# A feed-forward kernel's second matmul by one level of Strassen's algorithm: seven half-size products on summed blocks for eight

## The chip, the core and the metric

The kernel runs on one core of one Trainium2 chip. The metric is device time in microseconds, the median over executions. The profile names the engines PE (TensorE, matmul; PEld is its weight load), DVE (VectorE), ACT (ScalarE), POOL (GpSimd) and SP (SyncE, whose queue issues most DMAs here). Each engine works through its own instructions in order and waits on semaphores for the others.

## What is computed

```python
def _attn_ref(q, k, v):                 # (8, 8, 576, 64) each
    q_s = softmax of q over the head dimension
    k_s = softmax of k over the sequence
    kv = np.einsum('bhsd,bhse->bhde', k_s, v)
    return np.einsum('bhsd,bhde->bhse', q_s, kv)

def _moe_ref(x, w_in, w_out):           # x (4608, 512), w_in (512, 2048), w_out (2048, 512)
    h = x @ w_in
    g = 0.5 * h * (1.0 + erf(h / sqrt(2)))
    return g @ w_out
```

The attention's output, heads side by side, is x: 8 batches of 576 tokens, 512 wide. Inputs and output are fp32 in HBM; the kernel computes in bf16 with fp32 sums in PSUM.

## The kernel before

The tokens go in nine **chunks** of M = 512: chunks 0 to 7 are the first 512 tokens of each batch, chunk 8 the 64 that are left over of each. A chunk has three matmul parts on TensorE:

- **x**: `x_mm` multiplies the normalized queries, transposed (`qT`), with the batch's small matrix `kvc`; four copies (`x_evac`, two on ACT, two on DVE) put x, transposed, into `xT`.
- **h**: `h_phase` makes 16 tiles of h, transposed (128 of the 2048 hidden columns by 512 tokens), each of four matmuls of 512 columns (L348); ACT writes its GELU into `g` (L354), `[128, 16, 512]` bf16. `g` has one buffer.
- **y**: `y_phase` goes over four groups `j` of 128 tokens. For each, 16 matmuls of 512 columns (L376) sum over the hidden tiles `t`, with a block of `g` as weights and a row block of `wo_bf` (w_out in bf16) streaming. DVE copies each bank out (`y_out`, L384) and SP stores it. For chunk 8 the last group is done by `y_last` in 384 and 128 columns (L401), and its stores go out in halves of 64 rows, by SP and ACT.

The order of instructions on every engine is the order in the source (a manual schedule). What prepares a later chunk is put between matmuls of the y phase by the dict `ins`, whose keys are `(j, t)`. In chunks 2 to 5 the y phase of chunk c holds, for the batch nb = c + 2: `cast_v_all(nb)` (four DVE casts of V, L169) at (0, 8); `norm_q(nb)` at (1, 0), which is a reduce and a reciprocal on DVE and a multiplication on POOL (L245); `xbar_step(nb)` at (3, 0), a transposing DMA on SP's queue that makes `qT`; and at (2, 12) `x_all(c + 1)`, the x part of the next chunk, and `kv_step(nb)`, the k-times-v matmuls (L206) and their normalization on DVE. ACT does the exponentials of batch nb in the y phase as well. The loads of q, k and v for nb are issued by SP at the start of the h phase of chunk c. Chunk 6 has `norm_q` and the transpose only, for the left-over queries; chunks 7 and 8 prepare nothing but x for chunk 8.

The first part is written out by hand: weights are loaded in fp32 into five rotating buffers (`wst`) and cast to bf16 by DVE, POOL and ACT while chunk 0 runs; chunk 0's y phase is interleaved with the attention of batch 1, and the first four h tiles of chunk 1 are written out (`hps`). POOL's work there is casts and half of `norm_q(1)`.

PSUM has eight banks: three rotate for h (`psum_h`), two for y (`psum_y`), one (`a`) and a pair (`a2`) serve the attention.

Of the kernel before, what the change touches and what calls it, by code (L numbers as in the profile page):

```python
# [16 lines left out]
def kernel(  # L17
# [308 lines left out]
    def x_all(b):

        for hp in range(HP):
            pool, tag = (psum_h, "h") if hp < 3 else (psum_a, "a")
            x_tile(b, hp, pool, tag)  # L330
# [12 lines left out]
    def h_begin(c):  # L343
        st[c]["g"] = moe_sb.tile([128, NDF, M], BF16, tag="g", name="g", bufs=1)

    def h_mm(c, ps, t, dms):
        for dm in dms:
            nc.tensor.matmul(  # L348
                ps, wi_bf[:, dm, t * 128:(t + 1) * 128], st[c]["xT"][:, dm, :],
                start=(dm == 0), stop=(dm == NDM - 1),  # L350
            )
# [23 lines left out]
    def y_mm(c, ps, j, t):  # L375
        nc.tensor.matmul(  # L376
            ps, st[c]["g"][:, t, j * 128:(j + 1) * 128], wo_bf[:, t, :],
            start=(t == 0), stop=(t == NDF - 1),
        )

    def y_out(c, ps, j, eng="v"):
        y_sb = moe_sb.tile([128, DM], FP32, tag="y_sb")
        if eng == "v":
            nc.vector.tensor_copy(out=y_sb, in_=ps)  # L384
        else:
            nc.scalar.copy(out=y_sb, in_=ps)
        if c < B:
            dst = out[c * S:c * S + M, :].rearrange("(p j) n -> p j n", j=J)[:, j, :]
            nc.sync.dma_start(out=dst, in_=y_sb)
        else:  # L390
            for b2 in range(2):
                r0 = (2 * j + b2) * S + M
                nc.sync.dma_start(out=out[r0:r0 + R, :], in_=y_sb[b2 * R:(b2 + 1) * R, :])

    def y_last():

        j = J - 1
        for i, (c0, n) in enumerate(((0, 384), (384, 128))):
            ps = psum_y.tile([128, DM], FP32, tag="y")
            for t in range(NDF):  # L400
                nc.tensor.matmul(  # L401
                    ps[:, 0:n], st[B]["g"][:, t, j * 128:(j + 1) * 128],
                    wo_bf[:, t, c0:c0 + n], start=(t == 0), stop=(t == NDF - 1),
                )
            y_sb = moe_sb.tile([128, DM], FP32, tag="y_sb")
            nc.vector.tensor_copy(out=y_sb[:, 0:n], in_=ps[:, 0:n])  # L406
            for b2 in range(2):
                r0 = (2 * j + b2) * S + M
                eng = nc.scalar if b2 else nc.sync
                eng.dma_start(  # L410
                    out=out[r0:r0 + R, c0:c0 + n], in_=y_sb[b2 * R:(b2 + 1) * R, 0:n]
                )

    def y_phase(c, ins):
        for j in range(J - 1 if c == B else J):
            ps = psum_y.tile([128, DM], FP32, tag="y")
            for t in range(NDF):
                y_mm(c, ps, j, t)
                for f in ins.get((j, t), []):
                    f()  # L420
            y_out(c, ps, j)
        if c == B:
            y_last()
# [301 lines left out]
```

## Time and profile before

| what | us |
|---|---|
| median of 3 runs (279.41 to 279.45) | 279.44 |
| span of the profiled execution | 277.5 |
| PE busy in that span | 270.9 |
| one h phase, 64 matmuls of 512 columns | 13.81 |
| one y phase of chunks 2 to 5, with x and kv | 15.12 |
| y phase of chunk 1 (58.09 to 74.02) | 15.93 |
| y phase of chunk 8 to the end of the span (260.23 to 277.5) | 17.3 |

The profile is of one execution; its own time runs from its first to its last instruction, and the runs' median lies 1.94 us above that span. The granted TensorE clock is full in all slices of the page. A row of a group reads: line, engine, operation, output from input, shapes, count, then busy time and the mean of one, then the idle time of the engine just before and who ended it. A row of the timeline reads: start, duration, engine, line and operation, and in brackets how long the engine had been idle and for whom. In the chain, a row is start, length, what ran. Names are the program's; `e` is the exponential of q, `f` a loaded fp32 tile, `ps` a PSUM bank.

### The profile page before, as it was taken

The page shows a single profiled execution, that of the slowest core. Times are in us where ns is not written, and L with a number is a line of the kernel's source. Part 1 is how long each engine was busy: PE and PEld are TensorE (multiplying, and loading weights), DVE is VectorE, ACT ScalarE, POOL GpSimd, SP SyncE. Part 2 cuts the span into 40 slices and gives each one's busy share as a digit, 9 for nine tenths or more (in the row PEclk, how much of TensorE's full clock was granted, in tenths as well). Part 3 has the DMA queues.
Part 4 walks back from the last instruction along what each step waited for, and adds up shares of the span by engine and source line. Part 5 has one row for each costly group of instructions (what it writes and reads, how often), then busy time and mean ns, then how long its engine had stood idle before and what let it go on. Part 6 is the DMA issues. An engine that isn't in the chain of part 4 may idle for free.

```text
span 277.5 us, 4658 instructions
## 1 busy us (share of the span) xinstructions
PE 270.9 (98%) x1966; PEld 125.6 (45%) x1966; DVE 100.8 (36%) x154; ACT 158.9 (57%) x247; POOL 32.5 (12%) x26
## 2 busy tenths in 40 slices
PE   7799999999999999999999999999999999999995
PEld 3344454444444444444444444444444444444443
DVE  2876565319743540263008400751015200120012
ACT  4867686689377717791669246943683363126400
POOL 1520041002020310013000500050005000000000
PEclk9999999999999999999999999999999999999999
DMA  7999999974993249613981189117402500220033
GB/s 258 400 374 427 402 400 404 400 271 116 312 307 64 77 109 297 239 40 94 268 320 38 53 215 398 56 41 193 109 0 78 151 0 0 78 76 0 2 76 77
DMA packets 44980, 50.10 MB, mean 181 GB/s; under 512 B 20384, under 2 KB 29856, under 8 KB 44704
## 3 DMA queue, kind: packets, MB, share of 16 engines
q1 hardware_dynamic: 44560, 49.39, 53.5%
q10 hardware_dynamic: 400, 0.43, 0.5%
q8 instruction: 15, 0.25, 0.4%
q14 instruction: 5, 0.04, 0.1%
HBM read 36.70 MB, written 9.44 MB: 166 GB/s over the span
## 4 chain that ended last, share of the span: by engine, by line
PE 94%; DMA 4%; POOL 0%; DVE 0%; issue 0%; SPq 0%
PE ps L348 44%; PE ps L376 44%; DMA f<-in_v_dram 2%; PE kv L206 2%; PE ps L315 2%; DMA f<-in_q_dram 2%; PE ps L401 1%; PE pair L348 1%; POOL v_aug L169 0%; PE ps L320 0%; PE tp L279 0%; SPq L103 0%; DVE kvc L225 0%; DVE y_sb L406 0%; DVE rec L224 0%
## 5 line engine op out<-in xcount | busy, mean ns | idle before, releaser
L348 PE MATMUL ps<-xT,wi_bf 128*128 128x512 bf16 x568 | 124.9, 379 | 0.0
L376 PE MATMUL ps<-wo_bf,g 128*128 128x512 bf16 x560 | 124.1, 379 | 0.0
L354 ACT ACTIVATE g<-ps 128x512 bf16<-128x512 f32 x142 | 83.5, 598 | 66.8 <-PE ps L348 66.7
L348 PEld LDWEIGHTS <-wi_bf 128*128 128x128 bf16 x576 | 56.2, 98 | 68.0 <-issue 0.8
L376 PEld LDWEIGHTS <-g 128*128 128x128 bf16 x560 | 54.0, 98 | 64.6 <-issue 0.4
L384 DVE COPY y_sb<-ps 128x512 f32<-128x512 f32 x33 | 22.7, 687 | 81.0 <-PE ps L376 80.7
L245 POOL TENSOR_TENSOR e<-e,recq 128x2048 bf16<-128x2048 bf16 (+1 forms) x9 | 25.7, 2855 | 175.9 <-DVE recq L244 141.2
L169 DVE CAST v_aug<-f 128x576 bf16<-128x576 f32 x24 | 16.4, 746 | 48.3 <-DMA f<-in_v_dram 48.3
L243 DVE TENSOR_REDUCE qsum<-e 128x16 f32<-128x1024 bf16 (+1 forms) x13 | 21.1, 1622 | 13.7 <-ACT e L152 13.6
L341 ACT CAST xT<-ps 128x512 bf16<-128x512 f32 x18 | 9.9, 588 | 26.4 <-PE ps L315 15.9
L152 ACT ACTIVATE e<-f 128x512 bf16<-128x512 f32 (+1 forms) x42 | 20.5, 556 | 3.5 <-DMA f<-in_q_dram 3.5
L157 ACT ACTIVATE ek<-f 128x2304 bf16<-128x2304 f32 (+1 forms) x10 | 17.2, 1728 | 0.6 <-DMA f<-in_k_dram 0.5
L339 DVE CAST xT<-ps 128x512 bf16<-128x512 f32 x17 | 11.0, 687 | 17.1 <-PE ps L315 14.1
L79 ACT ACT_TABLE_LOAD x9 | 11.5, 1283 | 2.8 <-issue 2.7
L494 PE MATMUL ps<-zeros 128*128 128x512 f32 x14 | 8.0, 734 | 1.5 <-DVE zeros L520 1.5
L152 ACT ACT_TABLE_LOAD x7 | 9.0, 1283 | 0.1
L453 DVE CAST wi_bf<-w 128x512 bf16<-128x512 f32 x12 | 7.1, 621 | 1.8 <-DMA w<-in_moe_w_in_dram 1.4
L206 PEld LDWEIGHTS <-ek 64*64 64x64 bf16 x576 | 6.4, 105 | 2.2 <-issue 0.6
L206 PE MATMUL kv<-v_aug,ek 64*64 64x65 bf16 x576 | 6.8, 193 | 0.5 <-POOL v_aug L169 0.5
L487 DVE CAST wo_bf<-w 128x2048 bf16<-128x2048 f32 (+1 forms) x5 | 4.5, 907 | 6.1 <-DMA w<-in_moe_w_out_dram 6.1
L245 DVE TENSOR_TENSOR e<-e,recq 128x1024 bf16<-128x1024 bf16 x4 | 6.2, 1544 | 0.1
L315 PE MATMUL ps<-qT,kvc 64*64 64x512 bf16 x62 | 5.4, 390 | 0.3 <-DVE kvc L225 0.3
(40 smaller groups left out, 48.2 us busy)
## 6 DMA issues: line engine op xcount, KB each, us to landing
out_dram<-y_sb SPq DMA_DIRECT2D x32, 256.0 KB, 2.4
f<-in_k_dram SPq DMA_DIRECT2D x6, 1152.0 KB, 9.9
f<-in_v_dram SPq DMA_DIRECT2D x6, 1152.0 KB, 11.7
f<-in_q_dram SPq DMA_DIRECT2D x6, 1024.0 KB, 7.7
w<-in_moe_w_in_dram SPq DMA_DIRECT2D x6, 512.0 KB, 8.6
f<-in_v_dram SPq DMA_DIRECT2D x8, 288.0 KB, 6.5
f<-in_q_dram SPq DMA_DIRECT2D x4, 512.0 KB, 8.9
w<-in_moe_w_out_dram SPq DMA_DIRECT2D x2, 1024.0 KB, 11.4
```

What stands on the lines that cost most here:

```text
L79: nc.scalar.activation(out=scr[:, 1:2], in_=scr[:, 0:1], func=func)
L152: nc.scalar.activation(out=dst[:, i], in_=src[:, u], func=AF.Exp)
L157: nc.scalar.activation(out=ek[b % 2][:, i:i + n], in_=st[b]["kf"][:, i:i + n].rearrange("p x (n d) -> p x n d", n=NS), func=AF.Exp,)
L169: eng.tensor_copy(out=o, in_=i)
L206: nc.tensor.matmul(st[b]["kv"][hp][c, 0:D + 1], ek[b % 2][pr, hp, n, :], v_aug[b % 2][pr, hp, n, 0:D + 1], start=(n == 0), stop=(n == NS - 1),
L243: nc.vector.reduce_sum(out=qsum, in_=eq[:, :, hs, :], axis=AX.X)
L245: eng.tensor_tensor(out=eq[:, :, hs, :], in0=eq[:, :, hs, :], in1=recq.unsqueeze(3).to_broadcast([128, J, w, D]), op=ALU.mult,)
L339: nc.vector.tensor_copy(out=st[b]["xT"][:, hp, :], in_=ps)
L348: nc.tensor.matmul(ps, wi_bf[:, dm, t * 128:(t + 1) * 128], st[c]["xT"][:, dm, :], start=(dm == 0), stop=(dm == NDM - 1),)
L354: nc.scalar.activation(out=st[c]["g"][:, t, :], in_=ps, func=AF.Gelu)
L376: nc.tensor.matmul(ps, st[c]["g"][:, t, j * 128:(j + 1) * 128], wo_bf[:, t, :], start=(t == 0), stop=(t == NDF - 1),)
L384: nc.vector.tensor_copy(out=y_sb, in_=ps)
```

## The change

Chunk 0 stays as it was. From chunk 1 on, y = g times w_out is cut into 2 by 2 blocks (tokens 0 to 255 and 256 to 511, hidden tiles 0 to 7 and 8 to 15, output columns 0 to 255 and 256 to 511). With A the blocks of g and B those of w_out, the seven products are:

1. (A11 + A22)(B11 + B22), 2. (A21 + A22) B11, 3. A11 (B12 - B22), 4. A22 (B21 - B11), 5. (A11 + A12) B22, 6. (A21 - A11)(B11 + B12), 7. (A12 - A22)(B21 + B22)

and C11 = 1 + 4 - 5 + 7, C12 = 3 + 5, C21 = 2 + 4, C22 = 1 - 2 + 3 + 6. In `y_phase` they run in the order 4, 5, 1, 6, 2, 3, 7, each as 2 groups of 128 tokens by 8 hidden tiles, matmuls of 256 columns: 112 a chunk. PSUM adds 4 and 2, 5 and 3, and 1 and 7 (after 1 was read); the other sums are made by DVE, for chunks 1 to 7 two of them by POOL, and two copies by ACT. The keys of `ins` now say after which of the seven products a step comes.

The sums of w_out are made once, from the fp32 loads, on POOL (`mix_wo`); two of them replace quarters of `wo_bf` after chunk 0 has used them. The sums of g are made in every h phase by `s_ops`, four instructions for two pairs of tiles: for pairs 0 to 3 on POOL (on DVE in chunk 1), for pairs 4 to 7 on DVE. To have pairs early, the h tiles run in the order 8, 0, 9, 1 and so on (`h_pairs`). Differences of `g` overwrite two of its quarters.

`qT` and `xT` have one buffer each instead of two. Output goes out in pairs of token groups, 512 KB a store; in chunk 8 in pieces of 64 rows. `x_all` uses the pair `a2`, a bank that the y phase holds for it, and `a`; so `kv_step` now shares the pair with x.

```diff
+    w7 = singles.tile([128, HK, HN], BF16)
+    s12 = singles.tile([128, HK, M], BF16)
+    s5 = singles.tile([128, HK, HT], BF16)
...
-            st[b]["qT"] = attn_sb.tile([128, J, HP, 128], BF16, tag="qT", name="qT")
+            st[b]["qT"] = attn_sb.tile([128, J, HP, 128], BF16, tag="qT", name="qT", bufs=1)
...
+    def x_all(b, ps):
+
+        two = psum_a.tile([128, 2, M], FP32, tag="a2", name="xx")
+        for hp in range(2):
+            st[b][f"x{hp}"] = two[:, hp]
...
+        st[b]["x2"] = ps
+        x_tile(b, 3, psum_a, "a")
         x_mm(b, 0)
         x_mm(b, 1)
-        for hp, eng in ((0, "s"), (2, "v"), (1, "s"), (3, "v")):
+        for hp, eng in ((0, "s"), (1, "v"), (2, "s"), (3, "v")):
             x_evac(b, hp, eng)
...
+    def s_ops(c, p0, n, eng):
+
+
+        g = st[c]["g"]
+        a, b = slice(p0, p0 + n), slice(p0 + HK, p0 + HK + n)
+        lo, hi = slice(0, HT), slice(HT, M)
+        tt = eng.tensor_tensor
+        tt(out=s5[:, a], in0=g[:, a, lo], in1=g[:, b, lo], op=ALU.add)
+        tt(
+            out=s12[:, a].rearrange("p k (u m) -> p k u m", u=2),
+            in0=g[:, a].rearrange("p k (u m) -> p k u m", u=2),
+            in1=g[:, b, hi].unsqueeze(2).to_broadcast([128, n, 2, HT]), op=ALU.add,
+        )
+        tt(out=g[:, a, hi], in0=g[:, a, hi], in1=g[:, a, lo], op=ALU.subtract)
+        tt(out=g[:, b, lo], in0=g[:, b, lo], in1=g[:, b, hi], op=ALU.subtract)
+
+    def h_pairs(c, ins, done=(), eng=nc.gpsimd):
...
+        for p in range(HK):
+            for t in (p + HK, p):
+                if t in done:
+                    continue
+                ps = psum_h.tile([128, M], FP32, tag="h", name="ps")
+                h_mm(c, ps, t, range(NDM))
+                h_gelu(c, ps, t)
+            if p in (1, 3):
+                s_ops(c, p - 1, 2, eng)
+            elif p in (5, 7):
+                s_ops(c, p - 1, 2, nc.vector)
+            for f in ins.get(p, []):
+                f()
...
+        act = {
+            1: s12[:, :, lo], 2: s12[:, :, hi], 3: g[:, up, lo], 4: g[:, dn, hi],
+            5: s5, 6: g[:, up, hi], 7: g[:, dn, lo],
+        }
+        wgt = {
+            1: w16[:, 0], 2: wo_bf[:, up, 0:HN], 3: wo_bf[:, up, HN:DM],
+            4: wo_bf[:, dn, 0:HN], 5: wo_bf[:, dn, HN:DM], 6: w16[:, 1], 7: w7,
+        }
...
+        def mm(m, ps, first, final, ps2=None):
+            for j in range(2):
+                bank = ps2 if j and ps2 is not None else ps
+                own = bank is not ps
+                for k in range(HK):
+                    nc.tensor.matmul(
+                        bank[:, j * HN:(j + 1) * HN], act[m][:, k, j * 128:(j + 1) * 128],
+                        wgt[m][:, k, :], start=(first and k == 0 and (j == 0 or own)),
+                        stop=(k == HK - 1), skip_group_check=True,
+                    )
...
+        mm(4, bd, True, False)
+        after(0)
+        nc.vector.tensor_copy(out=f, in_=bd)
+        mm(5, be, True, False)
+        tt(f, f, be, ALU.subtract)
+        after(1)
+        mm(1, ba, True, False, ba2 if last else None)
...
+            tt(c22, two(f), two(ba))
+        after(2)
+        mm(6, bb, True, True)
+        tt(c22, c22, two(bb))
+        after(3)
+        mm(2, bd, False, True)
+        nc.scalar.copy(out=c21, in_=two(bd))
+        after(4)
+        mm(3, be, False, True)
+        nc.scalar.copy(out=c12, in_=two(be))
+        eng = nc.vector if last else nc.gpsimd
+        tt(c22, c22, c12, eng=eng)
+        tt(c22, c22, c21, ALU.subtract, eng=eng)
+        after(5)
+        y_store(c, 1, ysb[1])
+        if not last:
+            mm(7, ba, False, True)
+            tt(c11, two(f), two(ba))
+            y_store(c, 0, ysb[0])
+        else:
+            for j in range(2):
+                y_store_rest(j, ysb[0][:, j], HN, DM)
+            mm(7, ba, False, True, ba2)
+            for j, ps in enumerate((ba, ba2)):
+                n = slice(j * HN, (j + 1) * HN)
+                tt(c11[:, j], f[:, n], ps[:, n])
+                y_store_rest(j, ysb[0][:, j], 0, HN, (nc.sync, nc.scalar))
+        after(6)
...
+    w16 = None
+
+    def mix_wo(m, a, eng):
+
+
+        u, d = wo[a], wo[2 + a]
...
+        o, i0, i1, op = {
+            1: (w16[:, 0, k], u[:, :, lo], d[:, :, hi], ALU.add),
+            6: (w16[:, 1, k], u[:, :, lo], u[:, :, hi], ALU.add),
+            7: (w7[:, k], d[:, :, lo], d[:, :, hi], ALU.add),
+            3: (wo_bf[:, k, hi], u[:, :, hi], d[:, :, hi], ALU.subtract),
+            4: (wo_bf[:, k2, lo], d[:, :, lo], u[:, :, lo], ALU.subtract),
+        }[m]
+        eng.tensor_tensor(out=o, in0=i0, in1=i1, op=op)
...
     cast_wo(2, wo[2])
+    w16 = wst.tile([128, 2, HK, HN], BF16, tag="w", name="w16")
+    mix_wo(6, 0, nc.gpsimd)
+    mix_wo(6, 1, nc.gpsimd)
+    mix_wo(1, 0, nc.gpsimd)
...
     cast_wo(3, wo[3], 3, 1)
+    mix_wo(7, 0, nc.gpsimd)
+    mix_wo(1, 1, nc.gpsimd)
+    mix_wo(7, 1, nc.gpsimd)
...
+    for m in (4, 3):
+        for a in range(2):
+            mix_wo(m, a, nc.gpsimd)
+    h_pairs(1, {2: [lambda: cast_v_all(2)]}, done=t1s, eng=nc.vector)
...
-        (0, 15): [lambda: norm_q(2, 0, 2)],
-        (1, 1): [lambda: norm_q(2, 1, 2, nc.vector)],
-        (1, 14): [lambda: kv_step(2)],
-        (1, 15): [lambda: xbar_step(2)],
-        (2, 2): [lambda: cast_v_all(3), lambda: load(4)],
-        (3, 5): [lambda: x_all(2), lambda: kv_step(3)],
+        1: [lambda: norm_q(2, 0, 2), lambda: norm_q(2, 1, 2, nc.vector)],
+        2: [lambda: kv_step(2)],
+        3: [lambda: xbar_step(2), lambda: cast_v_all(3), lambda: load(4)],
+        5: [lambda: x_all(2, st[1]["xps"])],
+        6: [lambda: kv_step(3)],
...
-            yi[(1, 0)] = [lambda nb=nb: norm_q(nb)]
+            yi[1] = [lambda nb=nb: norm_q(nb)]
             if nb < B:
-                yi[(0, 8)] = [lambda nb=nb: cast_v_all(nb)]
-            yi[(3, 0)] = [lambda nb=nb: xbar_step(nb)]
+                yi[0] = [lambda nb=nb: cast_v_all(nb)]
         if c < B:
-            w = [lambda c=c: x_all(c + 1)]
+            yi[3] = [lambda c=c: x_all(c + 1, st[c]["xps"])]
+        if nb <= B:
+            yi[4] = [lambda nb=nb: xbar_step(nb)]
             if nb < B:
-                w.append(lambda nb=nb: kv_step(nb))
-            yi[(2, 12)] = w
+                yi[5] = [lambda nb=nb: kv_step(nb)]
```

More of the change, by code (lines that the diff above doesn't have):

```diff
@@ L68 @@
     kvc = [singles.tile([128, HP, D], BF16, name=f"kvc{b}") for b in range(B)]
-    zeros = singles.tile([128, 512], BF16)
     zeros32 = singles.tile([128, 512], FP32)
     scr = singles.tile([128, 2], FP32)
+    HK = NDF // 2
+    HT = M // 2
+    HN = DM // 2
+    w7 = singles.tile([128, HK, HN], BF16)
+    s12 = singles.tile([128, HK, M], BF16)
+    s5 = singles.tile([128, HK, HT], BF16)
     def setup_tiles():
@@ L285, in tp_quarters_evac @@
         if r == 0:
-            st[b]["qT"] = attn_sb.tile([128, J, HP, 128], BF16, tag="qT", name="qT")
+            st[b]["qT"] = attn_sb.tile([128, J, HP, 128], BF16, tag="qT", name="qT", bufs=1)
         o = st[b]["qT"].rearrange("p j x m -> p x j m")[:, :, :, r * 64:r * 64 + 64]
@@ L293, in xbar_step @@
     def xbar_step(b):
-        st[b]["qT"] = attn_sb.tile([128, J, HP, 128], BF16, tag="qT", name="qT")
+        st[b]["qT"] = attn_sb.tile([128, J, HP, 128], BF16, tag="qT", name="qT", bufs=1)
         nc.sync.dma_start_transpose(
@@ L301, in x_tile @@
         if "xT" not in st[b]:
-            st[b]["xT"] = attn_sb.tile([128, HP, M], BF16, tag="xT", name="xT")
+            st[b]["xT"] = attn_sb.tile([128, HP, M], BF16, tag="xT", name="xT", bufs=1)
         st[b][f"x{hp}"] = pool.tile([128, M], FP32, tag=tag, name="ps")
@@ L324, in x_mm @@
                         )
[L326 to L330, printed above, removed]
+    def x_all(b, ps):
+        two = psum_a.tile([128, 2, M], FP32, tag="a2", name="xx")
+        for hp in range(2):
+            st[b][f"x{hp}"] = two[:, hp]
+        if "xT" not in st[b]:
+            st[b]["xT"] = attn_sb.tile([128, HP, M], BF16, tag="xT", name="xT", bufs=1)
+        st[b]["x2"] = ps
+        x_tile(b, 3, psum_a, "a")
         x_mm(b, 0)
         x_mm(b, 1)
-        for hp, eng in ((0, "s"), (2, "v"), (1, "s"), (3, "v")):
+        for hp, eng in ((0, "s"), (1, "v"), (2, "s"), (3, "v")):
             x_evac(b, hp, eng)
@@ L354, in h_gelu @@
         nc.scalar.activation(out=st[c]["g"][:, t, :], in_=ps, func=AF.Gelu)
+    def s_ops(c, p0, n, eng):
[12 more added lines that the diff above has]
+    def h_pairs(c, ins, done=(), eng=nc.gpsimd):
+        if not done:
+            h_begin(c)
+        for p in range(HK):
[11 more added lines that the diff above has]
+                f()
     def h_phase(c, ins, groups={}, banks={}, t1=0):
@@ L381, in y_out @@
     def y_out(c, ps, j, eng="v"):
-        y_sb = moe_sb.tile([128, DM], FP32, tag="y_sb")
+        if j % 2 == 0:
+            st[c]["ysb"] = moe_sb.tile([128, 2, DM], FP32, tag="y_sb", name="y_sb", bufs=2)
+        y_sb = st[c]["ysb"]
         if eng == "v":
-            nc.vector.tensor_copy(out=y_sb, in_=ps)
+            nc.vector.tensor_copy(out=y_sb[:, j % 2], in_=ps)
         else:
-            nc.scalar.copy(out=y_sb, in_=ps)
+            nc.scalar.copy(out=y_sb[:, j % 2], in_=ps)
+        if j % 2:
+            y_store(c, j // 2, y_sb)
@@ L387, in y_out, with y_store @@
+    def y_store(c, half, y_sb):
+        j = 2 * half
         if c < B:
-            dst = out[c * S:c * S + M, :].rearrange("(p j) n -> p j n", j=J)[:, j, :]
+            dst = out[c * S:c * S + M, :].rearrange("(p j) n -> p j n", j=J)[:, j:j + 2, :]
             nc.sync.dma_start(out=dst, in_=y_sb)
         else:
[L391 to L412, printed above, removed]
@@ L414, in y_phase, with y_store_rest @@
-    def y_phase(c, ins):
[L415 to L423, printed above, removed]
+            for i in range(2):
+                y_store_rest(j + i, y_sb[:, i], 0, DM)
+    def y_store_rest(j, y_sb, c0, c1, engs=None):
+        for b2 in range(2):
+            r0 = (2 * j + b2) * S + M
+            eng = engs[b2] if engs else nc.sync
+            eng.dma_start(out=out[r0:r0 + R, c0:c1], in_=y_sb[b2 * R:(b2 + 1) * R, c0:c1])
@@ new lines, in y_phase, with two, tt, after @@
+    def y_phase(c, ins):
+        g = st[c]["g"]
+        lo, hi = slice(0, HT), slice(HT, M)
+        up, dn = slice(0, HK), slice(HK, NDF)
+        act = {
[6 more added lines that the diff above has]
+        }
+        last = c == B
+        bd = psum_y.tile([128, DM], FP32, tag="y", name="yd")
+        be = psum_y.tile([128, DM], FP32, tag="y", name="ye")
+        bb = psum_h.tile([128, DM], FP32, tag="h", name="yb")
+        st[c]["xps"] = psum_h.tile([128, DM], FP32, tag="h", name="yx")
+        ba = psum_h.tile([128, DM], FP32, tag="h", name="ya")
+        ba2 = st[c]["xps"] if last else ba
+        ysb = [moe_sb.tile([128, 2, DM], FP32, tag="y_sb", name="y_sb", bufs=2) for i in range(2)]
+        c11, c12 = ysb[0][:, :, 0:HN], ysb[0][:, :, HN:DM]
+        c21, c22 = ysb[1][:, :, 0:HN], ysb[1][:, :, HN:DM]
+        f = zeros32
+        def two(ps):
+            return ps.rearrange("p (j n) -> p j n", j=2)
+        def tt(out, in0, in1, op=ALU.add, eng=nc.vector):
+            eng.tensor_tensor(out=out, in0=in0, in1=in1, op=op)
+        def mm(m, ps, first, final, ps2=None):
[8 more added lines that the diff above has]
+                    )
+        def after(i):
+            for fn in ins.get(i, []):
+                fn()
+        mm(4, bd, True, False)
[5 more added lines that the diff above has]
+        mm(1, ba, True, False, ba2 if last else None)
+        if last:
+            for j, ps in enumerate((ba, ba2)):
+                n = slice(j * HN, (j + 1) * HN)
+                tt(c22[:, j], f[:, n], ps[:, n])
+        else:
[18 more added lines that the diff above has]
+            y_store(c, 0, ysb[0])
+        else:
+            for j in range(2):
+                y_store_rest(j, ysb[0][:, j], HN, DM)
+            mm(7, ba, False, True, ba2)
+            for j, ps in enumerate((ba, ba2)):
+                n = slice(j * HN, (j + 1) * HN)
+                tt(c11[:, j], f[:, n], ps[:, n])
+                y_store_rest(j, ysb[0][:, j], 0, HN, (nc.sync, nc.scalar))
+        after(6)
@@ L489, in cast_wo, with warm @@
             nc.scalar.copy(out=o, in_=w)
-    def warm(n, z=zeros):
+    w16 = None
+    def mix_wo(m, a, eng):
+        u, d = wo[a], wo[2 + a]
+        lo, hi = slice(0, HN), slice(HN, DM)
+        k = slice(4 * a, 4 * a + 4)
+        k2 = slice(HK + 4 * a, HK + 4 * a + 4)
+        o, i0, i1, op = {
[6 more added lines that the diff above has]
+        eng.tensor_tensor(out=o, in0=i0, in1=i1, op=op)
+    def warm(n, z):
         ps = psum_y.tile([128, DM], FP32, tag="y")
@@ L520 @@
     nc.vector.memset(zeros32, 0.0)
-    nc.vector.memset(zeros, 0.0)
     setup_tiles()
@@ L628 @@
     h_begin(1)
+    t1s = (HK, 0, HK + 1, 1)
     hps = [psum_h.tile([128, M], FP32, tag="h", name="ps") for t in range(2)]
@@ L631 @@
     for t in range(2):
-        h_mm(1, hps[t], t, (0, 1))
+        h_mm(1, hps[t], t1s[t], (0, 1))
     y_out(0, yps[2], 2, "s")
@@ L640 @@
     for t in range(2, 4):
-        h_mm(1, hps[t], t, (0, 1))
+        h_mm(1, hps[t], t1s[t], (0, 1))
     for t in range(4):
-        h_mm(1, hps[t], t, (2, 3))
-        h_gelu(1, hps[t], t)
-    h_phase(1, {12: [lambda: cast_v_all(2)]}, t1=4)
+        h_mm(1, hps[t], t1s[t], (2, 3))
+        h_gelu(1, hps[t], t1s[t])
+    for m in (4, 3):
+        for a in range(2):
+            mix_wo(m, a, nc.gpsimd)
+    h_pairs(1, {2: [lambda: cast_v_all(2)]}, done=t1s, eng=nc.vector)
     exp_q(2, parts=2)
@@ L677 @@
             ins[0] = [load_qrest]
-        h_phase(c, ins, groups={0: 2} if c == 2 else {})
+        h_pairs(c, ins)
         yi = {}
```

## The prediction

> **What bounds the kernel now.** First the page: shares of the engines, the chain of waits, the costliest group.
>
> ```profile
> PE 270.9 (98%) x1966; PEld 125.6 (45%) x1966; DVE 100.8 (36%) x154; ACT 158.9 (57%) x247; POOL 32.5 (12%) x26
> ...
> PE 94%; DMA 4%; POOL 0%; DVE 0%; issue 0%; SPq 0%
> ...
> L376 PE MATMUL ps<-wo_bf,g 128*128 128x512 bf16 x560 | 124.1, 379 | 0.0
> ```
>
> TensorE is busy 98% of the span and is 94% of the chain; the second matmul never waits (0.0 idle). Then the chain in order of time, chunk 4:
>
> ```profile
> 145.69 9.71 PE ps L376 x45
> 155.40 0.56 PE ps L315 x8
> 155.96 0.64 PE kv L206 x70
> 156.59 4.21 PE ps L376 x19
> 160.80 13.81 PE ps L348 x64
> ```
>
> 64 matmuls of 512 columns take 13.81 us (216 ns each); a y phase is 9.71 + 4.21 = 13.92 of matmul, plus x 0.56 and kv 0.64: 15.12. So fewer columns through TensorE are time, as long as nothing else makes it wait. What else runs in that phase I read from the timeline:
>
> ```profile
> 146.12 2.73 DVE L169 CAST v_aug<-f 128x576 bf16<-128x576 f32 x4 [13.52 <-DMA f<-in_v_dram]
> ...
> 149.85 2.29 DVE L243 TENSOR_REDUCE qsum<-e 128x32 f32<-128x2048 bf16 x1
> ...
> 152.25 0.35 DVE L244 RECIPROCAL recq<-qsum 128x32 f32<-128x32 f32 x1
> ...
> 156.00 1.29 DVE L339 CAST xT<-ps 128x512 bf16<-128x512 f32 x2 [2.68 <-PE ps L315]
> ```
>
> DVE already does 2.73 + 2.29 + 0.35 + 1.29 us and four copies of 0.69 there, and V lands only 0.43 us into the phase.
>
> **Price of the new matmuls.** No group has 256 columns, but the old last tile has 16 of 384 and 16 of 128, mean 256. The timeline of the end:
>
> ```profile
> 270.63 0.69 DVE L384 COPY y_sb<-ps 128x512 f32<-128x512 f32 x1 [2.76 <-PE ps L376]
> 273.23 0.56 DVE L406 COPY y_sb<-ps 128x384 f32<-128x384 f32 x1 [1.91 <-PE ps L401]
> 273.81 1.11 SPq L410 DMA_DIRECT2D out_dram<-y_sb  x2
> ...
> 274.12 0.29 DVE L406 COPY y_sb<-ps 128x128 f32<-128x128 f32 x1 [0.33 <-PE ps L401]
> ```
>
> Each copy starts when its group ends: 2.60 us for 16 of 384, 0.89 for 16 of 128 (56 ns each). So 256 columns cost 3.49/32 = 109 ns. New y phase: 7 x 16 x 0.109 = 12.2 us, 1.75 per product, against 13.92; about 0.1 of that is the handover from the h phase and stays, so 1.6 us a chunk is to be had, 12.8 in eight.
>
> [...]
>
> **What the change adds, and who hides it.** Of the 12.8 us I take back what DVE, POOL and SP can't do in time. T is the start of a y phase.
>
> Sums of g (s_ops): four two-input instructions per two tile pairs, of 512, 1024, 512, 512 elements. POOL: the rows of L245 give 1.90 us for 1024 and 3.62 for 2048, so 0.18 + 1.68 ns an element: 5.0 us a set. DVE: no row has two bf16 tensors in SBUF. Upper bound, the two-input row with an fp32 operand, 1.23 for 1024 (below): 3.1 us a set. Lower, the bf16 copies of L289, 0.69 for 1024: 1.8. I take 1.8: rows with fp32 in them take 1.2 to 1.3 ns an element (casts of 512 in 0.69, L245), those bf16 copies 0.67, and here all is bf16.
>
> DVE and POOL collide. Two stretches of the timeline, the first:
>
> ```profile
> 35.01 1.90 POOL L245 TENSOR_TENSOR e<-e,recq 128x1024 bf16<-128x1024 bf16 x1 [19.70 <-DVE recq L244]
> ...
> 36.30 1.69 DVE L245 TENSOR_TENSOR e<-e,recq 128x1024 bf16<-128x1024 bf16 x1
> ```
>
> and the second, where POOL is all but done when DVE starts:
>
> ```profile
> 62.99 1.90 POOL L245 TENSOR_TENSOR e<-e,recq 128x1024 bf16<-128x1024 bf16 x1 [20.22 <-DVE recq L244]
> ...
> 64.81 1.23 DVE L245 TENSOR_TENSOR e<-e,recq 128x1024 bf16<-128x1024 bf16 x1
> ```
>
> The same DVE instruction took 1.69 and 1.23 us, and in the first it ended 1.08 us after POOL's: a two-input DVE instruction stands still while POOL runs one. So s_ops on POOL and on DVE take turns.
>
> *Chunks 2 to 5.* POOL's sets 1 and 3 start 4.1 us into the h phase and need 10 us, past T-2.8, where DVE's set 5 is ready. Taking turns, set 5 ends near T+2.1 and set 7 at T+3.8 (alone: 2.5). The new order queues behind it on DVE: V casts 2.73, copy of the fourth product 0.69, subtraction of the fifth 0.69, reduce 2.29, reciprocal 0.35, two additions of 0.69, the copy of x1 0.69: 8.8, so x1 leaves PSUM at 12.7 (with gaps). kv_step takes that bank (a2) and now stands before the seventh product: TensorE is there at 6 x 1.75 + 0.56 + 0.1 = 11.2 and waits 1.6. y ends at 12.8 + 0.64 + 1.75 = 15.2 instead of 15.12. Loss 0.1 each, **-0.4**; with DVE alone and no collision, 13.9, a gain of 1.2. SP: the transposing DMA waits for the norm on POOL, both 512 KB stores come just ahead of the next load, about 1 us later in the h phase than now and with 0.75 MB more in front; at the 0.3 MB/us of that stretch V lands near T+3, just hidden by set 7.
>
> *Chunks 6 and 7.* No V cast and no kv: DVE's chain ends before TensorE needs it. **+3.0**.
>
> *Chunk 1.* Here POOL makes seven sums of w_out from 42.8 (end of its V casts), 1.90 each by the 1024 row, and all four sets are DVE's. Set 1 (ready at 49) takes turns with four sums until 56.5, then V casts 2.73, set 3, set 5, and set 7's first result at 63.2; the fifth product wants it at 58.1 + 1.75 + 0.65 = 60.5 and waits 2.7. All of DVE is late next: set 7 ends at T+6.5, then copy, subtraction, two reduces of 1.21 with reciprocals of 0.25, and the norm's DVE half, held by POOL's, ends at T+12.4. The transposing DMA (3.8 to landing) lands at 16.2; TensorE has come to x at 13.9 and waits; then x 0.56, the seventh product 1.75 and kv 0.64: y lasts 19.2, before 15.93. **-3.3** (bounds: +0.2 if nothing collides, -6.9 at DVE's slow rate).
>
> *Chunk 8.* TensorE is done at T+12.3, but the output is queued on SP. The lower right quarter needs the third product (T+10.5), a copy on ACT 0.59 and two fp32 additions of 0.69: T+12.9. Behind it SP issues 4 + 4 stores of 64 rows, then its two of the last quarter:
>
> ```profile
> L393 SPq DMA_DIRECT2D out_dram<-y_sb x6: 467/570/588, 264.4 to 271.9; - x6
> ```
>
> 4 x 0.6 + 4 x 0.5 + 0.5 brings the last issue to T+17.8. Before, it stood at 274.44 = T+14.2 with the span's end 3.1 later (T+17.3). Now T+20.8: **-3.5** (at the 0.34 of the 128-row stores: -1.6).
>
> Hidden at no cost: w_out sums before chunk 1 (POOL idle for 19.70 us there; uncovered, 5.7 us), the single buffers of qT and xT (readers done phases earlier), paired stores (buffers free a phase ahead).
>
> **Sum.** -3.3 - 0.4 + 3.0 - 3.5 = -4.2: span 277.5 + 4.2 = 281.7. The runs' median lies 1.94 above this execution's span, so 283.6.
>
> **Rivals.** [...] *Everything hidden:* 266.6; against it the kv bank alone. *Far slower:* two-input bf16 runs no faster than the fp32 row (3.1 a set): set 7 ends 2.6 later, chunk 1 -6.9, chunks 2 to 5 -2.7 each, 6 and 7 nothing (the fifth product waits 1.5), 8 -5: 302. [...]
>
> **How the numbers follow.** Forecast, 280 to 287.5: 48%. Faster: 28%, a quarter of it below 275. Within 0.2% (0.56 us, about what a measurement of this kernel can tell): 5%. Far slower: 19%, half above 291. So 283.6; 274.8 to 291.5 leaves out some 17%. Of the slower cases alone: 280 to 291.
>
> **What will show it.** Right: L376's successor at 109 ns pitch; TensorE waits for xT in chunks 2 to 5 at kv, for s5 in chunk 1; DVE two-input instructions stretched beside POOL; stores at the end back to back on SP for 4 us or more. Wrong: a pitch above 115 ns, no waits at kv, or an end within 4 us of the last matmul.

## The result, and the profile after

| what | us |
|---|---|
| median before, on the same chip | 279.44 (279.41 to 279.55) |
| median after, 4 runs | 291.02 (290.42 to 291.76) |
| ratio | 1.0414, 95% interval 1.0394 to 1.0434 |
| span of the profiled execution, before and after | 277.5 and 289.6 |

The change makes the kernel 4.1% slower: +11.6 us where +4.2 was forecast. The page of after, with the shares of the engines, the shares of the chain, and the groups of the sums of g (line, engine, operation, shapes, count, then busy time and mean ns, then idle time before and its releaser):

```profile
PE 261.4 (90%) x2314; PEld 161.5 (56%) x2334; DVE 172.4 (60%) x236; ACT 168.3 (58%) x263; POOL 158.8 (55%) x106
...
PE 54%; DVE 33%; DMA 5%; ACT 3%; issue 2%; POOL 0%; DVEq 0%; SPq 0%; ACTq 0%
...
L374 DVE TENSOR_TENSOR s<-g 128x512 bf16<-128x512 bf16 x18 | 19.2, 1069 | 70.6 <-ACT g L365 70.6
...
L375 POOL TENSOR_TENSOR s<-g 128x1024 bf16<-128x1024 bf16 x14 | 29.9, 2136 | 0.0
```

TensorE's busy time fell by 9.5 us, 270.9 to 261.4, of the 12.8 that Strassen takes away. But the span grew, and the chain that TensorE held at 94% now lies 33% on DVE. What TensorE waited for, in all (us, times, longest):

```profile
PE ye L492 <- DVE s L374: 7.8, 10, 1.3
PE kv L213 <- DVE xT L350: 4.2, 4, 1.1
...
PE xx L322 <- DMA qT<-e: 2.3, 1, 2.3
```

These three rows make 14.3 us, and before there were none of them. `ye` is the bank of the fifth product, the first that needs `s5`. Chunk by chunk, from the starts of the h and y phases in the chain of waits:

| part | before | after | change | forecast |
|---|---|---|---|---|
| up to y of chunk 1 | 58.09 | 58.29 | +0.2 | 0 |
| y of chunk 1 | 15.93 | 22.25 | +6.3 | +3.3 |
| chunk 2, h and y | 28.93 | 29.99 | +1.1 | +0.1 |
| chunks 3, 4, 5, each | 28.92 | 29.36 | +0.4 | +0.1 |
| chunks 6 and 7 | 56.68 | 55.00 | -1.7 | -3.0 |
| chunk 8 to the end | 31.09 | 35.98 | +4.9 | +3.5 |

**Chunk 3, a y phase of the common kind.** Its chain in order of time (start, length, what ran); T, its first product, is at 124.35:

```profile
120.93 0.61 ACT g L365
121.56 2.18 DVE s L374
123.74 1.57 DVE s L375
125.41 1.19 DVE g L380
...
128.66 2.64 DVE v_aug L176 x4
...
136.62 0.61 DVE xT L350
137.27 0.77 PE kv L213 x71
138.04 1.85 PE ya L492 x16
```

For 16 us the chain hardly leaves DVE, though TensorE has plenty to do: DVE is the queue that everything comes out of late. The first three DVE rows are set 5, which shares its time with POOL's set 3. The same stretch in the timeline shows what TensorE loses by it (brackets: idle before, and for whom):

```profile
127.32 1.26 PE L492 MATMUL ye<-wo_bf,s 128*128 128x256 bf16 x10 [0.58 <-DVE s L374]
...
137.27 0.77 PE L213 MATMUL kv<-v_aug,ek 64*64 64x65 bf16 x72 [1.03 <-DVE xT L350]
```

Two waits, 0.58 at the fifth product and 1.03 at kv, together 1.6 us: just the 1.6 that Strassen saves in a chunk. The y phase is 15.55 (124.35 to 139.90) against 15.12; the seven products at 1.75, x 0.56, kv 0.77 and the waits make 15.2 of it; 0.1 of the rest is the seventh product, which takes 1.85 behind kv, and the others are gaps where TensorE passes from one part to the next.

**Chunk 1.** Its timeline:

```profile
49.61 10.29 POOL L624 TENSOR_TENSOR wo_bf<-w 128x1024 bf16<-128x1024 f32 x4
...
49.87 2.83 DVE L375 TENSOR_TENSOR s<-g 128x1024 bf16<-128x1024 bf16 x1
...
52.73 2.46 DVE L380 TENSOR_TENSOR g<-g 128x512 bf16<-128x512 bf16 x1
...
55.11 2.56 DVE L381 TENSOR_TENSOR g<-g 128x512 bf16<-128x512 bf16 x1
...
64.17 1.26 PE L492 MATMUL ye<-wo_bf,s 128*128 128x256 bf16 x10 [1.34 <-DVE s L374]
...
75.57 0.41 PE L322 MATMUL xx<-qT,kvc 64*64 64x512 bf16 x4 [2.34 <-DMA qT<-e]
...
76.19 3.48 PE L492 MATMUL ya<-w,g 128*128 128x256 bf16 x16
```

POOL's last four sums of w_out run back to back; beside them one set of g takes DVE from 48.83 to 57.67, 8.8 us. The same four instructions later, with POOL still, take 0.34 + 0.61 + 0.43 + 0.34 = 1.7 us from start to start. The fifth product waits three times (0.46, 1.34, 1.34), x waits 2.34 for `qT`. The last row holds something that the forecast had no term for: the seventh product takes 3.42 us in the chain, where 1.75 was put. The stretches around it (length, then busy PE, PEld, DVE, ACT, POOL, then the granted clock of TensorE, DMA share, GB/s):

```profile
75.60:76.20 0.60, 0.60 (x9) 0.13 (x10) 0.25 (x1) 0.12 (x1) 0.60 (x1) 0.84 0.82 171
76.20:78.00 1.80, 1.80 (x12) 1.30 (x10) 1.29 (x2) 0.96 (x2) 0.39 (x1) 0.50 1.00 341
78.00:79.60 1.60, 1.60 (x9) 0.92 (x8) 0.00 (x0) 0.00 (x0) 0.00 (x0) 0.55 1.04 385
79.60:80.50 0.90, 0.78 (x73) 0.78 (x74) 0.75 (x2) 0.00 (x0) 0.00 (x0) 1.00 1.03 410
```

The granted clock is half from 76.0 to 79.4, the whole of that product. With a whole clock it takes 1.85 there (experiments 4 and 5), so the half clock costs 1.6 us.

**The end.** T of chunk 8 is 267.4; its timeline:

```profile
279.37 1.42 DVE L485 TENSOR_TENSOR y_sb<-y_sb 128x512 f32<-128x512 f32 x2 [3.47 <-ACT y_sb L523]
...
280.85 6.32 SPq L451 DMA_DIRECT2D out_dram<-y_sb  x10
281.15 1.19 ACTq L451 DMA_DIRECT2D out_dram<-y_sb  x2
```

The lower right quarter is summed at 280.78 (T + 13.4), and then SP issues ten stores in 6.32 us, 0.63 each, while TensorE is done at 280.4.

### The profile page after: what moved, and what is told of

It reads as the page before. It is cut to its first block, busy times and chain, and to the rows that moved or that the text cites. A ratio compares the mean times of both kernels' runs of the same rounds, so it can differ in the third digit from the quotient of the medians.

```text
span 289.6 us, 5574 instructions
## 1 busy us (share of the span) xinstructions
PE 261.4 (90%) x2314; PEld 161.5 (56%) x2334; DVE 172.4 (60%) x236; ACT 168.3 (58%) x263; POOL 158.8 (55%) x106
## 4 chain that ended last, share of the span: by engine, by line
PE 54%; DVE 33%; DMA 5%; ACT 3%; issue 2%; POOL 0%; DVEq 0%; SPq 0%; ACTq 0%
PE ps L359 30%; PE ya L492 7%; DVE s L374 6%; DVE s L375 6%; PE ps L422 5%; DVE g L380 5%; DVE v_aug L176 5%; PE ye L492 4%; DVE qsum L250 3%; DVE g L381 3%; PE yd L492 2%; PE yb L492 2%; DVE y_sb L485 2%; ACT g L365 2%; PE kv L213 2%; DMA f<-in_v_dram 2%
## 5 line engine op out<-in xcount | busy, mean ns | idle before, releaser
L374 DVE TENSOR_TENSOR s<-g 128x512 bf16<-128x512 bf16 x18 | 19.2, 1069 | 70.6 <-ACT g L365 70.6
L492 PEld LDWEIGHTS <-s 128*128 128x128 bf16 x384 | 36.3, 98 | 16.7 <-DVE s L374 10.6
L375 POOL TENSOR_TENSOR s<-g 128x1024 bf16<-128x1024 bf16 x14 | 29.9, 2136 | 0.0
L485 POOL TENSOR_TENSOR y_sb<-y_sb 128x512 f32<-128x512 f32 x14 | 17.7, 1267 | 15.5 <-ACT y_sb L523 14.9
L374 POOL TENSOR_TENSOR s<-g 128x512 bf16<-128x512 bf16 x14 | 16.9, 1208 | 15.1 <-ACT g L365 15.1
L492 PE MATMUL ye<-wo_bf,s 128*128 128x256 bf16 x128 | 17.0, 273 | 7.8 <-DVE s L374 7.8
L624 POOL TENSOR_TENSOR w<-w 128x1024 bf16<-128x1024 f32 x6 | 17.0, 2855 | 10.9 <-DMA w<-in_moe_w_out_dram 10.9
L375 DVE TENSOR_TENSOR s<-g 128x1024 bf16<-128x1024 bf16 x18 | 22.0, 1225 | 0.0
L381 POOL TENSOR_TENSOR g<-g 128x512 bf16<-128x512 bf16 x14 | 19.0, 1356 | 0.0
L380 POOL TENSOR_TENSOR g<-g 128x512 bf16<-128x512 bf16 x14 | 16.9, 1204 | 1.1
L492 PE MATMUL ya<-w,g 128*128 128x256 bf16 x120 | 16.0, 292 | 0.0
## 6 DMA issues: line engine op xcount, KB each, us to landing
f<-in_v_dram SPq DMA_DIRECT2D x6, 1152.0 KB, 11.6
```

The costliest lines, as they stand in the source:

```text
L374: tt(out=s5[:, a], in0=g[:, a, lo], in1=g[:, b, lo], op=ALU.add)
L375: tt(out=s12[:, a].rearrange("p k (u m) -> p k u m", u=2), in0=g[:, a].rearrange("p k (u m) -> p k u m", u=2), in1=g[:, b, hi].unsqueeze(2 ...
L380: tt(out=g[:, a, hi], in0=g[:, a, hi], in1=g[:, a, lo], op=ALU.subtract)
L381: tt(out=g[:, b, lo], in0=g[:, b, lo], in1=g[:, b, hi], op=ALU.subtract)
L485: eng.tensor_tensor(out=out, in0=in0, in1=in1, op=op)
L492: nc.tensor.matmul(bank[:, j * HN:(j + 1) * HN], act[m][:, k, j * 128:(j + 1) * 128], wgt[m][:, k, :], start=(first and k == 0 and (j == 0 ...
```

## The experiments

The two theories set against each other at the start were *turns* (POOL's and DVE's two-input instructions stand in each other's way, so all that queues on DVE is late) and *too much work* (DVE has more to do in the new kernel than TensorE's time hides, whoever does the sums of g). Each experiment ran beside the kernel before on the same chip; that median was 279.38 to 279.46 in all of them.

**1. All sums of g on DVE.** Turns would end, DVE's own work would grow.

```diff
-        h_pairs(c, ins)
+        h_pairs(c, ins, eng=nc.vector)
```

> All sums of g in chunks 2 to 8 on DVE, none on POOL. If the loss there is that DVE and POOL take turns on two-input instructions: no stretched DVE sums, set 7 ends near T+2.4 instead of T+4.3, TensorE's 0.58 us wait for s5 goes (7 chunks, 4.1 us) and the wait at kv shrinks from 1.03 to below 0.3 in chunks 2 to 5 (3 us), chunk 2's extra 0.7 too: about 283.5 us. If DVE simply has too much work in the y phase, 3.4 us more of it per chunk leaves the waits or lengthens them: 291 or more.

Measured: 281.52 (281.03 to 281.74), ratio 1.0067 (1.0052 to 1.0082): 9.5 us less than after, although DVE got eight more instructions in each of chunks 2 to 8. TensorE's waits, and one of the moved instructions (set 3 of chunk 3) in the timeline:

```profile
PE ye L492 <- DVE s L374: 3.4, 3, 1.3
...
PE xx L322 <- DMA qT<-e: 1.1, 1, 1.1
...
PE kv L213 <- DVE xT L350: 0.6, 2, 0.3
```

```profile
115.02 0.68 DVE L375 TENSOR_TENSOR s<-g 128x1024 bf16<-128x1024 bf16 x1
```

The wait at the fifth product is left in chunk 1 alone (3 times, 7.8 to 3.4 us), the one at kv is down from 4.2 to 0.6. DVE does in 0.68 us what took POOL 2.12. Too much work is out: more work on DVE, without POOL beside it, is ready sooner. Chunk 3 now lasts 27.93 us against 28.92 before the change, so here Strassen pays 1.0 us. Between the two profiled executions 9.2 us of the gain lie in chunks 2 to 8; another 1.2 lie in chunk 1, which the edit does not touch: there the half clock fell elsewhere and `qT` was waited for 1.1 instead of 2.3.

**2. The last stores on two queues.**

```diff
-            eng = engs[b2] if engs else nc.sync
+            eng = (nc.sync, nc.scalar)[b2]
```

> The 12 stores of chunk 8 alternate between SP and ACT (6 and 6) instead of 10 and 2. If the end is bound by SP issuing one store after another at 0.63 us: the last issue moves from 286.6 to about 284.1, 288.5 us in all. If the DMA engines' throughput bounds it: within 0.5 us of 291.0.

Measured: 289.12 (288.5 to 289.86), ratio 1.0334 (1.0315 to 1.0353), 1.9 us less than after.

```profile
281.31 3.77 SPq L451 DMA_DIRECT2D out_dram<-y_sb  x6
281.33 4.33 ACTq L451 DMA_DIRECT2D out_dram<-y_sb  x6
```

Two queues of six, instead of ten and two. The end was bound by the issuing, as said; the gain is smaller than expected because ACT's six took 4.33 us, 0.72 each.

**3. kv after the seventh product instead of before it**, so that TensorE does not stand at the bank that x1 leaves late.

```diff
-                yi[5] = [lambda nb=nb: kv_step(nb)]
+                yi[6] = [lambda nb=nb: kv_step(nb)]
```

> In chunks 2 to 5 kv_step stands after the seventh product instead of before it. If TensorE waits there for the bank that x1 leaves (1.03 us in chunks 2 to 5), the seventh product covers it: 4 us less, 287 us. If what is late is DVE as a whole, the wait moves to the h phase, which needs the last two quarters of xT: 290 to 291.

Measured: 287.7 (286.95 to 288.01), ratio 1.0287 (1.0268 to 1.0305), 3.3 less. The row of kv is gone from TensorE's waits, and the one at the fifth product has stayed:

```profile
PE ye L492 <- DVE s L374: 7.7, 10, 1.3
...
PE xx L322 <- DMA qT<-e: 1.5, 1, 1.5
```

**4. No sums of w_out beside chunk 1.** The last seven `mix_wo` on POOL are left out and the two tiles that would be read unset are zeroed; chunks 1 to 8 of the output are then not y.

```diff
-    mix_wo(7, 0, nc.gpsimd)
-    mix_wo(1, 1, nc.gpsimd)
-    mix_wo(7, 1, nc.gpsimd)
+    nc.gpsimd.memset(w7, 0.0)
+    nc.gpsimd.memset(w16[:, 0, 4:8], 0.0)
...
-    for m in (4, 3):
-        for a in range(2):
-            mix_wo(m, a, nc.gpsimd)
```

> The seven sums of w_out that POOL makes while chunk 1's h phase runs are left out (two of their outputs are set to zero instead), so the output of chunks 1 to 8 is not the reference's. If the taking of turns with POOL makes chunk 1 late: its first set of sums takes 1.8 us instead of 8.8, the waits in the fifth product (3.1 us) go, norm_q and the transposing DMA come some 5 us earlier, TensorE doesn't wait 2.3 us for them and its clock stays up (1.7 us): y of chunk 1 near 15.5 instead of 22.3, 284.5 us in all. If the new order of norm_q, transpose and x in chunk 1 is what costs: only the 3.1 us go, 288.

Measured: 286.2 (285.99 to 286.26), ratio 1.0236 (1.022 to 1.0251): 4.8 less than after.

```profile
49.19 0.69 DVE L375 TENSOR_TENSOR s<-g 128x1024 bf16<-128x1024 bf16 x1
...
64.70 0.78 PE L213 MATMUL kv<-v_aug,ek 64*64 64x65 bf16 x72 [1.15 <-ACT ek L164]
...
71.90 0.41 PE L322 MATMUL xx<-qT,kvc 64*64 64x512 bf16 x4 [1.07 <-DMA qT<-e]
72.46 1.92 PE L492 MATMUL ya<-w,g 128*128 128x256 bf16 x16
```

DVE's 2.83 became 0.69, the y phase 22.25 became 16.8 (58.3 to 75.08), and the seventh product takes 1.85 in the chain instead of 3.42. TensorE still waits 2.2 us, for ACT's exponential of k and for `qT`; the likely reason, which no run here tests, is the new order, in which kv(2) and x stand earlier against their makers than before. These waits are more than the 1.7 by which 4.8 falls short of the 6.5 expected. The run takes the sums away altogether, so it does not tell their longer time from the turns that they force on DVE.

**5. Dummy matmuls in chunk 1's waits.** If the half clock follows from TensorE's idling, filling the waits takes it away, although nothing arrives sooner.

```diff
...
+                    if c == 1 and m == 5 and j == 0 and k in (1, 3, 5):
+                        fill(2 if k == 1 else 6)
...
-        5: [lambda: x_all(2, st[1]["xps"])],
+        5: [lambda: fill(10), lambda: x_all(2, st[1]["xps"])],
```

(`fill(n)` is n matmuls of 512 columns whose result nothing reads.)

> In chunk 1, 14 matmuls of 512 columns whose results nobody reads fill TensorE's waits inside the fifth product (3.0 us of work for 3.1 of waits), 10 more fill the wait before x (2.2 for 2.3). The waits end when they did. If TensorE's clock falls to half because it idled there, it stays at 1.00 through the seventh product, which takes 1.75 instead of 3.42: 1.7 us less, 289.3. If the half clock has another cause, or the waits are what they are, 291.0 or somewhat more.

Measured: 290.02 (289.8 to 290.21), ratio 1.0378 (1.0365 to 1.0391), 1.0 less; the profiled span is 1.4 less. The window in which the seventh product runs, 76.36 on:

```profile
76.00:78.00 2.00, 2.00 (x23) 1.48 (x16) 1.13 (x3) 1.07 (x2) 0.80 (x1) 1.00 0.88 297
```

The clock is whole, and the product takes 1.85 us in the chain. The mean granted clock over the span says the same of all runs: 0.990 to 0.992 in these five, 0.980 to 0.985 in the four of after. Adding work to TensorE made the kernel faster. In after the granted clock fell to 0.50 at 76.0, 0.4 us behind a wait of 2.34 us that had shorter ones before it (0.46, 1.34, 1.34); how long an idling it takes, these runs do not show.

**6. Chunk 8 as before**, with one long sum and 128-row stores, wo_bf's two overwritten quarters being made again on POOL.

```diff
...
+        if c == B:
+            h_phase(c, ins)
+            for a in range(2):
+                nc.gpsimd.tensor_copy(out=wo_bf[:, 4 * a:4 * a + 4, HN:DM], in_=wo[a][:, :, HN:DM])
+                nc.gpsimd.tensor_copy(out=wo_bf[:, HK + 4 * a:HK + 4 * a + 4, 0:HN], in_=wo[2 + a][:, :, 0:HN])
+            y_plain(c, {})
+            continue
```

> Chunk 8's y phase is the one of before (16 matmuls of 512 columns a group, last group 384 and 128; four casts on POOL put the two quarters of wo_bf back during its h phase). If Strassen's tail (DVE's additions, then ten stores on SP) costs what the traces say, the chunk takes 31.1 us instead of 36.0: 286.1. If the new tail is slow for what comes before it, less is won: 288 to 291.

Measured: 286.21 (285.5 to 286.94), ratio 1.0242 (1.0225 to 1.0259): 4.8 less, nearly the whole +4.9 that the table gives to chunk 8. In its chain the chunk takes 31.2 us (253.96 to 285.16), against 35.98 in after and 31.09 before.

**7. Experiments 1, 2 and 3 in one kernel.** Are their gains one and the same, or do they add?

> Sums of g on DVE, chunk 8's stores on two queues and kv after the seventh product together. If the wait at kv is a late result of the taking of turns, kv last adds only the 0.3 us that are left at two places: 281.5 - 1.9 - 0.6 = 279.0. If the three are separate causes they add up: 291.0 - 9.5 - 1.9 - 3.3 = 276.3.

Measured: 279.09 (277.8 to 279.97, 12 runs), ratio 0.9984 (0.997 to 0.9998). The three gains alone are 9.5 + 1.9 + 3.3 = 14.7, together 11.9; of the 2.4 below experiment 1, the stores explain 1.9. The wait at kv was, for the most part, DVE's lateness seen a second time.

**8. Strassen in chunks 2 to 7 only**, sums of g on DVE, kv last, and the sums of w_out that replace quarters of `wo_bf` made in chunk 2's h phase. Chunks 1 and 8 are done in the old way.

```diff
...
-    h_pairs(1, {2: [lambda: cast_v_all(2)]}, done=t1s, eng=nc.vector)
+    h_phase(1, {12: [lambda: cast_v_all(2)]}, t1=4)
...
-    y_phase(1, {
+    y_plain(1, {
...
+    for m in (4, 3):
+        for a in range(2):
+            mix_wo(m, a, nc.gpsimd)
...
```

> Chunks 1 and 8 as before, chunks 2 to 7 by Strassen with all sums of g on DVE and kv after the seventh product; POOL makes the four sums that overwrite wo_bf during chunk 2's h phase. If the matmuls' price (1.75 a product) is what is left once the waits are gone: 1.2 us less than before in each of chunks 2 to 5, 1.6 in 6 and 7, about 1 given back in chunk 2: 272.3, faster than before by 2.5%. If more than the waits found so far stands in the way: 276 or more.

Measured: 273.29 (272.92 to 273.6), ratio 0.9779 (0.9766 to 0.9792). What is still lost, from chunk 3:

```profile
120.42 2.73 DVE L176 CAST v_aug<-f 128x576 bf16<-128x576 f32 x4 [2.12 <-DMA f<-in_v_dram]
...
123.81 1.91 PE L501 MATMUL yd<-wo_bf,s 128*128 128x256 bf16 x16 [0.46 <-DVE zeros L513]
```

V has become the last to come, 4.8 us into the y phase (in experiment 1 it came 3.0 into it; what delays it here is not traced): DVE stands 2.12 us for it, and the copy that empties the fourth product's bank is queued behind.

**9. One set of four on POOL instead of two**, to tell POOL's summing as such from its overlap with DVE.

```diff
-            if p in (1, 3):
+            if p == 1:
                 s_ops(c, p - 1, 2, eng)
-            elif p in (5, 7):
+            elif p in (3, 5, 7):
```

> In chunks 2 to 8 POOL keeps set 1 of the sums of g (it ends 9.7 us into the h phase, before DVE's set 5 is ready at 11.0), DVE takes set 3 too. If the loss is the overlap of two-input instructions on the two engines, it is nearly gone though POOL still makes sums: within 1 us of the run with all sums on DVE (281.5), a little above it, since set 3 on DVE (ready 7.5 us into the phase) still meets POOL once or twice, early in the phase where nothing waits. If it costs that POOL makes sums at all, half the gain is lost: 286.

Measured: 281.77 (281.61 to 282.36), ratio 1.0088 (1.0071 to 1.0105), as fast as with no set on POOL within the intervals, although one wait of 0.9 us at kv is left, in chunk 4.

```profile
115.10 1.15 POOL L380 TENSOR_TENSOR g<-g 128x512 bf16<-128x512 bf16 x1
115.19 1.34 DVE L374 TENSOR_TENSOR s<-g 128x512 bf16<-128x512 bf16 x1 [6.85 <-ACT g L365]
...
122.10 0.42 DVE L374 TENSOR_TENSOR s<-g 128x512 bf16<-128x512 bf16 x1 [1.41 <-ACT g L365]
```

Set 3 on DVE meets POOL (1.34 for 0.42), but early, where nothing waits; by the last set POOL is done. So what costs the time is that POOL's second set meets DVE's sets 5 and 7 at the end of the h phase.

**10. Experiment 8 with V cast one product later**, ahead of `norm_q` at key 1 instead of at key 0.

```diff
-                yi[0] = [lambda nb=nb: cast_v_all(nb)]
+                yi[1] = [lambda nb=nb: cast_v_all(nb), lambda nb=nb: norm_q(nb)]
```

> The kernel with chunks 2 to 7 by Strassen, with the V casts on DVE moved behind the copy of product 4 and the subtraction of product 5. In the run before, V landed 4.8 us into chunk 3's y phase, DVE stood still for 2.1 us with those two operations queued behind, and TensorE waited 0.46 us for the copy and 0.27 for the bank of product 7. If that is V's late load, these waits go in chunks 3 to 5: 272.0 or 1.3 us less at most; if DVE's amount of work binds, 273.3.

Measured: **271.24** (271.18 to 271.36), ratio 0.9707 (0.9693 to 0.9722): 2.05 us less than experiment 8, more than the 1.3 that were expected at most. The waits of 0.46 and 0.27 are gone; where the other 0.7 comes from is not traced. Shares and the granted clock in tenths over the span:

```profile
PE 263.6 (98%) x2254; PEld 153.6 (57%) x2254; DVE 154.6 (57%) x255; ACT 165.6 (61%) x259; POOL 79.5 (30%) x52
...
PEclk9999999999999999999999999999999999999999
```

TensorE is at 98% again, as before the change, with 7.3 us less to do. This version beats both kernels: 8.2 us under before, 19.8 under after.

## Why the prediction was right in direction and wrong in size

- **Price of the new matmuls: right.** A product of 16 matmuls is 1.75 us in the chain (`yb` and `yd` of chunk 8), so 109 ns each, as worked out from the old last tile. Busy time fell by 9.5 us where 12.8 was to be had; 1.6 of the difference is the seventh product of chunk 1 at half clock; the rest is not accounted for here.
- **Turns of DVE and POOL: right, and the main cause.** Some 9 us of the time lie in them (experiment 1). All the signs that the prediction named for being right are in the traces: the 109 ns, the waits at kv and for `s5`, DVE's stretched instructions, the stores back to back. The step that failed is the sizing. Too little was put for a set on POOL (5.0 us, measured 5.54) and for a sum of w_out (1.90, measured 2.33 alone and 2.57 with turns); the wait at the fifth product in chunks 2 to 8 (0.58 us, in chunk 2 1.19) and the half clock in chunk 1 (1.6) were put at nothing; and the issue of the last stores was put too short. The engines took turns an instruction each, as forecast (in chunk 3 of after POOL's instructions ended at 123.46, 124.76 and 126.32, DVE's at 123.74, 125.31 and 126.60), and the misses beyond the forecast lie in chunk 1 (3.0), in each of chunks 2 to 5 (0.3 to 1.0), in chunks 6 and 7 (1.3 together) and at the end (1.4).
- **Chunk 1, -3.3 forecast, -6.3 measured: the largest miss, 3.0 of 7.9 us.** The step "seven sums of w_out, 1.90 each by the 1024 row" took its price from a row of bf16 with one broadcast operand; these read two fp32 tiles. The first three, alone, took 6.98 / 3 = 2.33 us each, the last four with turns 10.29 / 4 = 2.57. POOL was done at 59.90 instead of 56.5, set 7's first result came at 64.11 instead of 63.2, the norm's DVE half ended at T + 13.2 instead of T + 12.4, and x ran at T + 17.3 instead of T + 16.2. The other half of the miss is the seventh product, 3.42 us where 1.75 was put: the half clock, for which the sum had no term. With x 1.1 later and that product 1.7 longer, 19.2 becomes 22.0 of the measured 22.25.
- **Chunks 2 to 5, -0.4 forecast, -2.4 measured.** DVE alone needs 1.7 us a set, as taken (1.8). The step "5.0 us a set on POOL" was 5.54 (114.69 to 120.23 in chunk 3). So set 7 ended at T + 4.3 instead of T + 3.8, and its first result came after TensorE wanted it: the 0.58 wait at the fifth product, in chunk 2 1.19, was left out of the sum for these chunks. The wait at kv was there, at 1.03 to 1.1 instead of 1.6, and experiments 1 and 7 show that it hangs on the same lateness. In chunks 3 to 5 the two waits together are the 1.6 that was put at kv alone, so there the total of the waits was right; the 0.35 by which each y phase is longer than the 15.2 forecast are kv (0.77 for 0.64), the seventh product (1.85 for 1.75) and x1 leaving its bank 0.1 later. Chunk 2 lost 1.1; its wait at the fifth product is 0.6 longer than theirs. V was just hidden, as forecast; in experiment 8, where it comes later, it becomes the limit.
- **Chunks 6 and 7, +3.0 forecast, +1.7 measured.** The same 0.58 in each; "DVE's chain ends before TensorE needs it" held for everything but the fifth product. With the sums on DVE the two chunks take 26.70 and 26.79 us, 1.6 less each than before: the forecast gain.
- **Chunk 8, -3.5 forecast, -4.9 measured.** The mechanism was right (experiments 2 and 6). The quarter came at T + 13.4 instead of T + 12.9, the fifth product's wait again. The stores took 0.63 each, where 0.6 and 0.5 were put, and the last was issued at 286.6, T + 19.2 instead of T + 17.8: the 1.4 that are missing.
- **Rivals.** *Everything hidden*, and with it the 28% for a faster kernel, fell with the turns. In experiment 7 set 7 is done at T + 2.5 in chunk 3, against T + 4.3 in after, and the kernel still takes 279.1: chunk 1 still loses about 6 us there. *Two-input bf16 no faster than the fp32 row* fell: 1024 elements in 0.68 us.

Left open: how long an idling it takes to bring the half clock on, why ACT's half of the stores takes 0.72 us each in experiment 2, and why V comes later in experiment 8.

## What to carry to other kernels

Here 9.5 us less of TensorE work came with 11.6 us more of time, because what feeds it was not ready sooner as well: see that Strassen's sums are done before the phase that they shorten, on an engine that nothing holds up. Splitting the sums of g over DVE and POOL where both run at once cost 9.5 us against DVE alone (291.0 and 281.5): give such sums to the faster one, and after each mend look for the next late producer (here the sums, then bank and stores, then V). Leave the stages without slack plain: six chunks of eight, so mended, gave 8.2 us, where all eight as first written cost 11.6.

## What the runs showed of the hardware

- **Two-input bf16 instructions on DVE that met one of POOL ended just behind it.** One of 0.42 us alone took 1.34 beside POOL's 1.15 (experiment 9) and 2.18 beside POOL's 2.12 (after, chunk 3), and ended 0.28 us behind POOL's both times; beside POOL's sums of w_out in chunk 1 it took 2.46 to 2.56. Where both queues were full they alternated, one instruction each (after, chunk 3, 121.3 to 126.6). The short instructions lost by far more: in chunk 1 DVE's four took 8.8 us for 1.7, POOL's four 10.29 for 9.3 (four at the 2.33 of those that ran alone). What the two engines contend for, no run shows.
- **POOL was slower than DVE at bf16 sums too:** 512 elements in 1.15 us, 1024 in 2.12 (after, chunk 3), against DVE's 0.42 and 0.68 (experiment 1).
- **The granted clock of TensorE fell to 0.50 in chunk 1, during or just behind short waits.** It was 0.50 for 3.4 us in after and in experiments 1, 2 and 7 (in 9 too, by the 1.7 us that its fifth and first products lost), and for 6.8 us in 3 and 6. In after and in 2 it began within 0.5 us of the end of the wait of 2.34 or 2.43 us before x; the three waits inside the fifth product (0.46 to 0.81, 1.34 and 1.34 us) had passed without it. In 1, 3, 6, 7 and 9 it began during nearly the same three waits (0.43 to 0.88, 1.34 and 1.34) or at most 0.8 us behind them. It did not come where the waits were filled but for 0.26 and 0.21 (5), absent (8 and 10), or 1.15 and 1.07 (4). So nearly the same idling came with the half clock in some executions and without it in others, and no threshold follows from these runs. The same stretch, first in after, then in experiment 1 (the granted clock is the third number from the end):

```profile
66.00:68.00 2.00, 2.00 (x85) 1.64 (x84) 1.90 (x3) 2.00 (x4) 0.00 (x0) 1.00 0.00 0
...
66.00:68.00 2.00, 2.00 (x12) 1.42 (x10) 1.90 (x3) 2.00 (x4) 0.00 (x0) 0.50 0.00 0
```

- **Stores of 64 rows left SP 0.63 us apart** (0.59 for the issue itself) in after; from ACT they came 0.60 apart in after and 0.72 in experiment 2.
